# Routed rows gathered a unit ahead, and one PSUM bank of the attention read by two engines

## The chip, the cores and the metric

The kernel runs on one core of one Trainium2 chip. The metric is device time in microseconds (us). Before the change three runs took 1354.52, 1353.81 and 1352.93 us, with a median of 1353.81 us. A separate profiled execution, from which every duration below is read, took 1352.68 us.

## The reference

One input `x` (2048 tokens of 448 numbers) goes through two branches that are mixed per token:

```python
g = _sigmoid((x * gate_w).sum(-1, keepdims=True))
a = _A_ref(x, A_wqkv, A_wo)          # attention, 16 heads of 28
b = _B_ref(x, B_w_gate, B_w1, B_w2)  # 8 experts, the 2 best of each token
return g * a + (1 - g) * b
```

`_A_ref` is full softmax attention over all 2048 keys with an output projection `wo`. `_B_ref` sends each token to two of eight experts (448 to 1792 to 448, with silu) and adds their results with softmax weights.

## The kernel before, in words

The program has four stages on one core. First q, k and v, the routing and the gate are computed. Then the eight experts run; beside them VectorE takes maxima of score tiles. The experts' results go to a tensor `ys_d` in HBM, in the order of the experts' slots. The third stage, from about 836 to 1311 us, is the attention itself. The fourth projects the attention's output with `wo`, adds the routed part and stores it.

The change is in the third stage. There are 16 units `u` (four groups of four heads, times four chunks of 512 queries), and each unit has 8 cells `p`, so 128 cells `m`. A cell handles two tiles of 128 keys for four heads: 8 score tiles of 128 x 512, each the size of one PSUM bank. The scores of cell 0 are made at the end of the expert stage, those of the other 127 by `scores` (L1161).

PSUM has eight banks of that size, and all are in use: two banks of three (`s0`, `s1`, from `triple`) and two single ones (`z0`, `z1`, from `single`). Each cell's `scores` fills, for its first key tile, a single bank and `s0`, and for its second the three banks of `s1` and the other single one. `z[0]` is the single bank of the first key tile, `z[1]` that of the second. ScalarE then computes `exp` into the tile `P` in SBUF: from `z[0]` (L1173), from `s0` (L1174) and from `s1` (L1176). VectorE copies `z[1]` to the SBUF tile `X` (L1175), and ScalarE takes its last `exp` from there (L1177).

`values(m)` (L1180) multiplies the 8 tiles of `P` with the values, 16 matmuls in the trace, into one single bank, and VectorE adds that bank to `osb` (L1192 for the first cell of a unit, L1194 for the others). The bank for this is `single(m + 1)`: the one that held `z[0]` of cell `m + 1`.

The order of each engine's instructions is the order in which the Python code issues them. The loop issues `scores(m + 1)`, then `beside(m)`, then `values(m)`. The tile framework adds the semaphore waits that the order of issue calls for. So on TensorE the scores of the next cell stand ahead of the values of this one, and on VectorE the copy to `X` of the next cell stands ahead of what `beside(m)` puts there and of the add to `osb`.

`beside(m)` spreads the small work over the cells of a unit. In cell 1 `fetch_routed(u)` (L1060) lets GpSimd gather, by two indirect DMAs, the two expert results of 128 tokens out of `ys_d` into `yg0` and `yg1` (two buffers each). `routed(u)` (L1073 to L1077) adds them on VectorE in four steps, in cells 2, 4, 5 and 6. In cell 0 GpSimd's queue also has `collect_sums` of the unit before, in cell 3 `invert_sums` and in cell 4 `spread_sums`; `divide` in cell 7 sends the finished rows to `OT` through SyncE's queue. `split_o` (three VectorE instructions: L1086, L180, L181) prepares tiles of `OT` for the projection; it runs in the cells listed in `WHOLE_O`, and the fourth tile is split by ScalarE after the loop.

Of the kernel before, what the change touches and what calls it, by code (L numbers as in the profile page):

```python
# [8 lines left out]
F32 = mybir.dt.float32  # L9
# [3 lines left out]
AF = mybir.ActivationFunctionType  # L13
# [36 lines left out]
SCALE = float(DH) ** -0.5  # L50
# [12 lines left out]
def tile_gated_mha_moe(ctx: ExitStack, tc: tile.TileContext, x, xe_, xT, wv, wqk, wo, w1, w2, out):  # L63
    nc = tc.nc
# [43 lines left out]
    def max_stream():  # L108
# [6 lines left out]
        while b < len(cells):  # L115
# [19 lines left out]
            if more:  # L135
                nc.vector.tensor_reduce(mp[:, o:o + 1], banks[0], axis=AX.X, op=ALU.max)  # L136
            o += more
# [3 lines left out]
            for lo, hi in zip(cuts, cuts[1:]):  # L141
                h = lo // 3
                nc.vector.tensor_reduce(mp[:, (o + lo) % 256:(o + lo) % 256 + hi - lo], pm[h][:, lo - 3 * h:hi - 3 * h],  # L143
                                        axis=AX.X, op=ALU.max)
            for n, (g, qt, kc, j) in enumerate(step):
                if kc == 3 and j == 3 and qt % 4 == 3:
# [3 lines left out]
                    nc.vector.tensor_reduce(mg[:, 0:16].rearrange("p (j t) -> p j t", j=4), part,  # L150
                                            axis=AX.X, op=ALU.max)
                    mr = mxp.tile([128, 32], F32, name="mr")
# [124 lines left out]
    with ExitStack() as pa:  # L277
        sb = pa.enter_context(tc.tile_pool(name="pa_sb", bufs=1))
# [148 lines left out]
        def tmp(name, shape, dt=F32):  # L427
            return sb.tile(shape, dt, name=name)
# [5 lines left out]
        def routing():  # L434
            Lx = L
            ms_, masks = [], []
            for tag in "12":
                m = tmp("m" + tag, [128, NT])
                nc.vector.tensor_reduce(m, Lx, axis=AX.X, op=ALU.max)
                yield  # L440
# [6 lines left out]
                mi = tmp("mi", [128, NT])  # L447
                nc.vector.tensor_reduce(mi, cand, axis=AX.X, op=ALU.min)
                yield
# [37 lines left out]
            pos = tmp("pos", [128, E])  # L487
            nc.vector.tensor_reduce(pos, ahead, axis=AX.X, op=ALU.add)
            yield
# [199 lines left out]
    def load_v(g, hf):  # L689
        t = cpool[hf].tile([128, NT // 2, 128], F32, name=f"V{hf}")  # L690
        nc.sync.dma_start(t, v_d[hf * 1024:(hf + 1) * 1024, g * 128:(g + 1) * 128]
                          .rearrange("(t p) d -> p t d", p=128))
        return t


    def load_k(g, hf):
        r = []
        cs = slice(hf * 1024, (hf + 1) * 1024)
        for part, src in (("h", qkh_d), ("l", qkl_d)):
            kt_ = cpool[hf].tile([128, 1024], F32R, name=f"K{part}{hf}")  # L700
            kf = kt_.bitcast(F32)
            for j in range(4):
                r0 = D + (4 * g + j) * DH
                nc.sync.dma_start(kf[32 * j:32 * j + DH].rearrange("p (c n) -> p c n", c=2),
                                  src[2 * hf:2 * hf + 2, r0:r0 + DH].rearrange("c r n -> r c n"))
                if part == "h":
                    nc.sync.dma_start(kf[32 * j + DH:32 * j + KR], neg_d[:, cs])
            r.append(kt_)
        return r


    def load_q(g, qc):
        need_max(g, qc)
        q = c0.tile([128, 2, 512], F32R, name="Q", bufs=2)
        qf = q.bitcast(F32)
        for i, src in enumerate((qkh_d, qkl_d)):
            for j in range(4):
                r0 = (4 * g + j) * DH
                nc.sync.dma_start(qf[32 * j:32 * j + DH, i], src[qc, r0:r0 + DH])
        for j in range(4):  # L720
            nc.sync.dma_start(qf[32 * j + DH:32 * j + KR, 0], m_d[4 * g + qc, j:j + 1])
        return q
# [4 lines left out]
    def score_passes(kt, keys, q, banks):  # L727
        kh, kl = keys
        ks = slice((kt % 8) * 128, (kt % 8 + 1) * 128)
        for i, (k, c, r) in enumerate(((kh, 0, KR), (kh, 1, DH), (kl, 0, DH))):  # L730
            for j in range(4):
                rw = slice(32 * j, 32 * j + r)
                nc.tensor.matmul(banks[j], k[rw, ks], q[rw, c], start=i == 0, stop=i == 2)  # L733
# [4 lines left out]
    with ExitStack() as pb:  # L738
        sb1 = pb.enter_context(tc.tile_pool(name="pb_sb1", bufs=2, reuse_waits="tile"))
        sb = pb.enter_context(tc.tile_pool(name="pb_sb", bufs=2, reuse_waits="tile"))  # L740
# [135 lines left out]
        def first_scores(n):  # L876
# [9 lines left out]
            for j in range(4):  # L886
                P = (mxp.tile([128, 512], F32R, name="khg", bufs=6) if 4 * n + j < 6 else
                     mxp.tile([128, 512], F32R, name="qg")).bitcast(F32)
                nc.scalar.activation(P, banks[j], AF.Exp, scale=SCALE)
                Ps[n].append(P)  # L890

# [8 lines left out]
        for e in range(E):  # L900
# [12 lines left out]
            for hf in range(2):  # L913
# [3 lines left out]
                for f in range(NH):  # L917
                    ft = hf * NH + f
                    p = e * NP + ft // 2
# [69 lines left out]
                for n_k, k in enumerate((4, 0, 1, 2, 3)):  # L989
# [7 lines left out]
                    n = 128  # L997
# [3 lines left out]
                    i = 0  # L1001
                    for f in range(NH if k < 4 else 0):
# [10 lines left out]
                        if hf == 1 and e + 1 < E and (f == 1 or f == 4 and n_k == 1):  # L1013
                            j = n_k if f == 1 and n_k > 1 else f // 4
# [27 lines left out]
    sb = ctx.enter_context(tc.tile_pool(name="pc_sb", bufs=2, reuse_waits="tile"))  # L1042
# [8 lines left out]
    def fetch_wo(b):  # L1051
        wo_r[b] = sb.tile([128, D], F32, name="wo_r")
        nc.sync.dma_start(wo_r[b], wo[:, b])

    def split_wo(b):
        w_ = wo_r[b]
        nc.vector.tensor_copy(wo_h[:, b], w_)
        nc.vector.tensor_tensor(wo_l[:, b], w_, wo_h[:, b].bitcast(F32), op=ALU.subtract)

    def fetch_routed(t):  # L1060
        yg = []
        for c in range(2):
            y = sb.tile([128, 2, D], F32, name=f"yg{c}")
            nc.gpsimd.indirect_dma_start(out=y.rearrange("p c d -> p (c d)"), out_offset=None, in_=ys_d,
                                         in_offset=bass.IndirectOffsetOnAxis(ap=slot_i[:, c, t:t + 1], axis=0))
            yg.append(y)
        ygs[t] = yg
# [40 lines left out]
    def collect_sums(u):  # L1108
        for j in range(4):
            nc.gpsimd.dma_start(sum_d[u, j:j + 1], accs[u][32 * j + DH:32 * j + DH + 1])  # L1110
        rc[u] = sb.tile([128, 16], F32, name="rc")
        nc.gpsimd.dma_start(rc[u], by_slices(sum_d[u]))

    def invert_sums(u):
        r = rc.pop(u)
        nc.vector.reciprocal(r, r)
        nc.gpsimd.dma_start(by_slices(inv_d[u]), r)
# [25 lines left out]
    NU = 4 * NG  # L1143
# [4 lines left out]
    Pc = {0: Ps[0] + Ps[1]}  # L1148

    def single(i):  # L1150
        return ps.tile([128, 512], F32, name=f"z{i % 2}")

    def triple(i):
        return ps.tile([128, 3, 512], F32, name=f"s{i}")
# [6 lines left out]
    def scores(m):  # L1161
        u, p = divmod(m, NPR)
        if p == 0 and u and u + 1 < NU:
            qs[u + 1] = load_q((u + 1) // 4, (u + 1) % 4)
        X = sb.tile([128, 512], F32, name="X")
        P = sb.tile([128, 8, 512], F32, name="P")
        z, t = [None] * 2, [None] * 2
        for i in range(2):
            kt = 2 * p + i
            z[i], t[i] = single(m + i), triple(i)  # L1170
            three = [t[i][:, j] for j in range(3)]
            score_passes(kt, held[u // 4][0][kt // 8], qs[u], three + [z[i]] if i else [z[i]] + three)
        nc.scalar.activation(P[:, 0], z[0], AF.Exp, scale=SCALE)  # L1173
        nc.scalar.activation(P[:, 1:4], t[0], AF.Exp, scale=SCALE)  # L1174
        nc.vector.tensor_copy(X, z[1])  # L1175
        nc.scalar.activation(P[:, 4:7], t[1], AF.Exp, scale=SCALE)  # L1176
        nc.scalar.activation(P[:, 7], X, AF.Exp, scale=SCALE)  # L1177
        Pc[m] = [P[:, i] for i in range(8)]

    def values(m):  # L1180
        u, p = divmod(m, NPR)
# [14 lines left out]
    def beside(m):  # L1196
        u, p = divmod(m, NPR)
        g, qc = divmod(u, 4)
        if qc == 3 and g + 1 < NG:
            if p == 3:  # L1200
                held[g + 1] = [load_k(g + 1, 0), None], [None, None]
            if p == 4:
                held[g + 1][1][0] = load_v(g + 1, 0)
            if p == 6:
                held[g + 1][0][1] = load_k(g + 1, 1)
        if g and qc == 0 and p == 0:
            held[g][1][1] = load_v(g, 1)
        if u and p == 0:
            collect_sums(u - 1)
        if p == 1:  # L1210
            fetch_routed(u)
        if p == 4 and 4 <= u < 8:
            fetch_wo(u - 4)
        if p == 0 and 5 <= u < 9:
            split_wo(u - 5)
        if (u, p) in WHOLE_O:
            split_o(WHOLE_O.index((u, p)), nc.vector)
        if u and p == 3:
            invert_sums(u - 1)
        if u and p == 4:  # L1220
            spread_sums(u - 1)
        if u and p == 7:
            divide(u - 1)
        if p in (2, 4, 5, 6):
            next(sums.setdefault(u, routed(u)))

    WHOLE_O = [(NU - 2, 1), (NU - 1, 0), (NU - 1, 1)]
    for m in range(NU * NPR):
        if m + 1 < NU * NPR:
            scores(m + 1)  # L1230
        beside(m)
        values(m)
# [70 lines left out]
```

## Time and profile before

| | before |
|---|---|
| median of three runs | 1353.81 us |
| the profiled execution | 1352.68 us, of which the span of its instructions is 1350.9 us |
| TensorE busy | 1341.4 us (99%) |
| VectorE busy | 928.1 us (69%) |
| ScalarE busy | 847.5 us (63%) |
| GpSimd busy | 616.6 us (46%) |
| mean granted TensorE clock | 0.998 of full speed |

Busy time is the time covered by an engine's records. Records of consecutive instructions overlap, on TensorE and on ScalarE alike, and the ends of matmuls are modelled; so a share of 99% does not say that the engine could do no more. In the rows below a start and a duration stand first, and the bracket behind an instruction tells how long its engine had been idle before it and what ended that. PE is TensorE, DVE is VectorE, ACT is ScalarE, POOL is GpSimd.

### The profile page before, as it was taken

The page shows a single profiled execution, that of the slowest core. Times are in us where ns is not written, and L with a number is a line of the kernel's source. Part 1 is how long each engine was busy: PE and PEld are TensorE (multiplying, and loading weights), DVE is VectorE, ACT ScalarE, POOL GpSimd, SP SyncE. Part 2 cuts the span into 40 slices and gives each one's busy share as a digit, 9 for nine tenths or more (in the row PEclk, how much of TensorE's full clock was granted, in tenths as well). Part 3 has the DMA queues.
Part 4 walks back from the last instruction along what each step waited for, and adds up shares of the span by engine and source line. Part 5 has one row for each costly group of instructions (what it writes and reads, how often), then busy time and mean ns, then how long its engine had stood idle before and what let it go on. Part 6 is the DMA issues. An engine that isn't in the chain of part 4 may idle for free. (4 is left out here: it accounts for less than half of the span.)

```text
span 1350.9 us, 27181 instructions
## 1 busy us (share of the span) xinstructions
PE 1341.4 (99%) x10166; PEld 887.2 (66%) x10166; DVE 928.1 (69%) x1076; ACT 847.5 (63%) x1270; POOL 616.6 (46%) x661
## 2 busy tenths in 40 slices
PE   9999999999999999999999999999999999999998
PEld 8888788788887777777777776434444444444348
DVE  5746898888988888988888775444445444444455
ACT  5325354355354343543435435999999999999881
POOL 2123775676587666875768752122222222222220
PEclk9999999999999999999999999999999999999999
DMA  9887856753453465534655313123322432432123
GB/s 344 306 272 263 301 156 192 239 160 104 154 157 104 143 192 160 161 97 144 187 154 162 102 39 103 42 62 106 103 77 71 131 100 58 109 103 70 48 58 129
DMA packets 136279, 191.30 MB, mean 142 GB/s; under 512 B 23285, under 2 KB 102681, under 8 KB 135633
## 3 DMA queue, kind: packets, MB, share of 16 engines
q1 hardware_dynamic: 124992, 160.55, 38.3%
q0 software_dynamic: 11008, 28.76, 7.1%
q8 instruction: 80, 1.31, 0.4%
q14 instruction: 55, 0.44, 0.1%
q10 hardware_dynamic: 144, 0.23, 0.1%
HBM read 139.20 MB, written 60.74 MB: 148 GB/s over the span
## 5 line engine op out<-in xcount | busy, mean ns | idle before, releaser
L143 DVE TENSOR_REDUCE mp<-pm 128x3 f32<-128x1536 f32 (+1 forms) x301 | 508.9, 1733 | 10.9 <-PE pm L122 10.9
L1188 PE MATMUL z<-P,V 128*32 128x512 f32 x2032 | 246.4, 602 | 0.0
L1176 ACT ACTIVATE P<-s 128x1536 f32<-128x1536 f32 x127 | 198.1, 1560 | 0.9 <-PE s L733 0.9
L1174 ACT ACTIVATE P<-s 128x1536 f32<-128x1536 f32 x127 | 196.5, 1547 | 0.0
L1175 DVE COPY X<-z 128x512 f32<-128x512 f32 x127 | 87.9, 692 | 150.2 <-PE z L733 142.1
L733 PE MATMUL s<-Q,Kh 29*128 29x512 f32 x1524 | 188.5, 444 | 0.0
L733 PE MATMUL z<-Q,Kh 29*128 29x512 f32 x508 | 185.5, 444 | 2.7 <-DVE osb L1194 2.7
L804 POOL TENSOR_TENSOR w2l<-w2r,w2h 128x448 fp32r<-128x448 f32 x112 | 129.3, 1156 | 117.9 <-ACT w2h L798 90.4
L1020 ACT ACTIVATE yo<-acc 128x448 f32<-128x448 f32 x64 | 34.8, 544 | 231.1 <-PE acc L1006 226.3
L1006 PE MATMUL acc<-w2h,hh 128*128 128x448 f32 x448 | 167.5, 374 | 0.3 <-PEq L818 0.3
L1006 PE MATMUL acc<-w2h,hl 128*128 128x448 f32 x448 | 166.4, 372 | 0.0
L1006 PE MATMUL acc<-w2l,hh 128*128 128x448 f32 x448 | 166.0, 371 | 0.0
L949 ACT ACTIVATE hf<-acc 128x512 f32<-128x512 f32 (+6 forms) x154 | 74.2, 482 | 138.0 <-PE acc L945 131.0
L733 PEld LDWEIGHTS z<-Q,Kh 29*128 29x128 f32 x508 | 74.5, 183 | 111.9 <-issue 30.2
L136 DVE TENSOR_REDUCE mp<-acc 128x1 f32<-128x512 f32 x130 | 89.5, 688 | 84.6 <-PE pm L122 81.6
L813 POOL TENSOR_TENSOR hl<-hf,hh 128x512 fp32r<-128x512 f32 x112 | 144.9, 1294 | 1.0 <-ACT hh L952 1.0
L1188 PEld LDWEIGHTS z<-P,V 128*32 128x32 f32 x2032 | 53.3, 109 | 129.7 <-issue 77.4
L945 PE MATMUL acc<-xeh,w1h 128*128 128x512 f32 (+3 forms) x408 | 136.8, 339 | 0.0
L945 PE MATMUL acc<-xeh,w1l 128*128 128x512 f32 (+3 forms) x408 | 136.0, 338 | 0.0
L1194 DVE TENSOR_TENSOR osb<-z,osb 128x512 f32<-128x512 f32 x112 | 77.4, 691 | 82.1 <-PE z L1188 81.9
L1110 POOL DMA_DIRECT2D sum_d<-osb x64 | 31.0, 492 | 202.8 <-DVE osb L1194 202.8
L772 POOL TENSOR_TENSOR w1l<-w1r,w1h 128x1024 fp32r<-128x1024 f32 (+1 forms) x49 | 90.9, 1854 | 61.1 <-ACT w1h L766 47.5
(221 smaller groups left out, 2779.1 us busy)
## 6 DMA issues: line engine op xcount, KB each, us to landing
w2r<-in_w_dram SPq DMA_DIRECT2D x112, 224.0 KB
w1r<-in_w_dram SPq DMA_DIRECT2D x56, 384.0 KB
ys_d<-zero_d SPq DMA_DIRECT2D x32, 448.0 KB
ys_d<-yo SPq DMA_DIRECT2D x64, 224.0 KB
x_d<-xf SPq DMA_DIRECT2D x115, 64.0 KB
qkh_d<-hi SPq DMA_DIRECT2D x28, 256.0 KB
qkl_d<-lo SPq DMA_DIRECT2D x28, 256.0 KB
w1r<-in_w_dram SPq DMA_DIRECT2D x112, 64.0 KB
```

The source lines that it names most:

```text
L136: nc.vector.tensor_reduce(mp[:, o:o + 1], banks[0], axis=AX.X, op=ALU.max)
L143: nc.vector.tensor_reduce(mp[:, (o + lo) % 256:(o + lo) % 256 + hi - lo], pm[h][:, lo - 3 * h:hi - 3 * h], axis=AX.X, op=ALU.max)
L733: nc.tensor.matmul(banks[j], k[rw, ks], q[rw, c], start=i == 0, stop=i == 2)
L772: nc.gpsimd.tensor_tensor(l[:, :, half], r[:, :, half], h[:, :, half].bitcast(F32), op=ALU.subtract)
L804: nc.gpsimd.tensor_tensor(w2l, w2r, w2h.bitcast(F32), op=ALU.subtract)
L813: nc.gpsimd.tensor_tensor(hl, hf32, hh[:, 0:512].bitcast(F32), op=ALU.subtract)
L945: nc.tensor.matmul(pu[:, 0:HC], a, b[:, cs], start=i == 0, stop=i == len(mms) - 1)
L1006: nc.tensor.matmul(py[:n, 0:D], a[:, cs], b, start=i == 0, stop=i == 3 * NH - 1)
L1174: nc.scalar.activation(P[:, 1:4], t[0], AF.Exp, scale=SCALE)
L1175: nc.vector.tensor_copy(X, z[1])
L1176: nc.scalar.activation(P[:, 4:7], t[1], AF.Exp, scale=SCALE)
L1188: nc.tensor.matmul(po[32 * j:32 * j + 32], v[:, kt % 8, 32 * j:32 * j + 32], P[4 * i + j], start=i == 0, stop=i == 1)
```

## The change

There are three edits, all in the attention stage.

1. `z[0]` of every cell is read by two engines. ScalarE takes `exp` of its columns 0 to 255 straight from the bank; VectorE copies its columns 256 to 511 to the front of `X`, which grows from 512 to 768 columns. The copy of `z[1]` goes behind it in `X`, and ScalarE's last `exp` takes all 768 columns of `X`. The order of issue is: ScalarE's `exp` of the half bank, VectorE's copy of the other half, the two `exp` of 1536 columns, VectorE's copy of `z[1]`, the last `exp`. `P` becomes one row of 4096 columns, in which columns 0 to 511 are the first score tile and columns 512 to 1023 the one that comes from `z[1]`.
2. The gathers of a unit are issued in cell 5 of the unit before, those of unit 0 ahead of the loop.
3. Three `split_o` move from cells (14, 1), (15, 0), (15, 1) to cells (15, 0), (15, 1), (15, 3), as (unit, cell).

```diff
-        X = sb.tile([128, 512], F32, name="X")
-        P = sb.tile([128, 8, 512], F32, name="P")
+        X = sb.tile([128, 768], F32, name="X")
+        P = sb.tile([128, 4096], F32, name="P")
...
-        nc.scalar.activation(P[:, 0], z[0], AF.Exp, scale=SCALE)
-        nc.scalar.activation(P[:, 1:4], t[0], AF.Exp, scale=SCALE)
-        nc.vector.tensor_copy(X, z[1])
-        nc.scalar.activation(P[:, 4:7], t[1], AF.Exp, scale=SCALE)
-        nc.scalar.activation(P[:, 7], X, AF.Exp, scale=SCALE)
-        Pc[m] = [P[:, i] for i in range(8)]
+        nc.scalar.activation(P[:, 0:256], z[0][:, 0:256], AF.Exp, scale=SCALE)
+        nc.vector.tensor_copy(X[:, 0:256], z[0][:, 256:512])
+        for i in range(2):
+            nc.scalar.activation(P[:, 1024 + 1536 * i:2560 + 1536 * i], t[i].rearrange("p j n -> p (j n)"),
+                                 AF.Exp, scale=SCALE)
+        nc.vector.tensor_copy(X[:, 256:768], z[1])
+        nc.scalar.activation(P[:, 256:1024], X, AF.Exp, scale=SCALE)
+        Pc[m] = [P[:, 512 * i:512 * i + 512] for i in (0, 2, 3, 4, 5, 6, 7, 1)]
...
-        if p == 1:
-            fetch_routed(u)
+        if p == 5 and u + 1 < NU:
+            fetch_routed(u + 1)
...
-    WHOLE_O = [(NU - 2, 1), (NU - 1, 0), (NU - 1, 1)]
+    fetch_routed(0)
+    WHOLE_O = [(NU - 1, 0), (NU - 1, 1), (NU - 1, 3)]
```

## Rows read from the trace of the kernel before

**Rows 1.** An undisturbed stretch of the attention as one window: its length, then the busy time of PE, PEld (weight loads), DVE, ACT and POOL with the number of instructions, the granted clock, the share of the DMA engines and GB/s.

```profile
1010.00:1200.00 190.00, 190.00 (x2072) 77.11 (x2068) 91.76 (x147) 190.00 (x208) 46.93 (x79) 1.00 0.35 96
```

**Rows 2.** ScalarE's instructions in order of time, in an undisturbed stretch of the attention.

```profile
1102.77 0.72 ACT L1173 ACTIVATE P<-z 128x512 f32<-128x512 f32 x1
1103.26 1.57 ACT L1174 ACTIVATE P<-s 128x1536 f32<-128x1536 f32 x1
1104.59 1.58 ACT L1176 ACTIVATE P<-s 128x1536 f32<-128x1536 f32 x1
1105.92 0.76 ACT L1177 ACTIVATE P<-X 128x512 f32<-128x512 f32 x1
1106.45 0.72 ACT L1173 ACTIVATE P<-z 128x512 f32<-128x512 f32 x1
...
1128.57 0.72 ACT L1173 ACTIVATE P<-z 128x512 f32<-128x512 f32 x1
```

**Rows 3.** TensorE and VectorE beside the same cell: the values, the copy to X, the first and the last matmul of the next z[0], the add to osb.

```profile
1103.54 1.92 PE L1188 MATMUL z<-P,V 128*32 128x512 f32 x16
1103.66 0.69 DVE L1175 COPY X<-z 128x512 f32<-128x512 f32 x1 [1.12 <-PE z L733]
1105.39 0.49 PE L733 MATMUL z<-Q,Kh 29*128 29x512 f32 x1
1105.53 0.69 DVE L1192 COPY osb<-z 128x512 f32<-128x512 f32 x1 [1.18 <-PE z L1188]
1105.96 0.39 PE L733 MATMUL z<-Q,Kl 28*128 28x512 f32 x1
```

**Rows 4.** All instructions of L1173 in the program: shortest, median and longest duration in ns, first and last start.

```profile
L1173 ACT ACTIVATE P<-z x127: 597/714/723, 835.9 to 1306.2; 128x512 f32<-128x512 f32 x127
```

**Rows 5.** Waits from 880 to 1320 us: engine, what waited, for whom, us in total, times, the longest in us. Below them the gathers' time from issue to landing, and one pair of gathers in GpSimd's order of time.

```profile
DVE yg L1073 <- DMA yg<-ys_d,slot_i: 6.5, 7, 2.0
DVE oh L1086 <- DMA OT<-osb: 2.1, 1, 2.1
...
DMA to landing us min/median/max: 4.1/4.9/6.9
...
960.17 0.97 POOL L1064 DMA_INDIRECT yg<-ys_d,slot_i  x1 [0.31 <-issue]
```

**Rows 6.** Two of those waits in order of time, and what follows on TensorE and ScalarE; below them the window in which the granted clock was lowest.

```profile
964.81 0.62 DVE L1073 TENSOR_TENSOR yg<-yg 128x448 f32<-128x448 f32 x1 [1.97 <-DMA yg<-ys_d,slot_i]
965.36 0.68 DVE L1194 TENSOR_TENSOR osb<-z,osb 128x512 f32<-128x512 f32 x1
966.09 0.49 PE L733 MATMUL z<-Q,Kh 29*128 29x512 f32 x1 [0.88 <-DVE osb L1194]
969.91 0.60 ACT L1173 ACTIVATE P<-z 128x512 f32<-128x512 f32 x1 [1.05 <-PE s L733]
...
1259.96 0.49 PE L733 MATMUL z<-Q,Kh 29*128 29x512 f32 x1 [1.85 <-DVE osb L1194]
1260.75 1.45 ACT L1176 ACTIVATE P<-s 128x1536 f32<-128x1536 f32 x1 [0.86 <-PE s L733]
1260.86 3.62 PE L1188 MATMUL z<-P,V 128*32 128x512 f32 x16
1265.46 0.60 ACT L1173 ACTIVATE P<-z 128x512 f32<-128x512 f32 x1 [2.74 <-PE s L733]
...
1261.00:1262.00 1.00, 1.00 (x8) 0.25 (x8) 0.96 (x2) 1.00 (x1) 0.00 (x0) 0.50 0.00 0
```

**Rows 7.** TensorE after the second of these waits: the first matmul of a cell's scores, and the values behind them.

```profile
1264.41 0.49 PE L733 MATMUL z<-Q,Kh 29*128 29x512 f32 x1
1266.18 1.92 PE L1188 MATMUL z<-P,V 128*32 128x512 f32 x16
```

**Rows 8.** The first stage, in order of time: ScalarE (L416) reads columns 0 to 447 of a PSUM bank, VectorE (L417) columns 448 to 456 of the same bank; the two pairs are of two banks.

```profile
14.37 0.55 ACT L416 ACTIVATE hi<-pq 128x448 f32<-128x448 f32 x1 [2.65 <-PE pq L371]
14.81 0.54 ACT L416 ACTIVATE lo<-pq 128x448 f32<-128x448 f32 x1
14.95 0.17 DVE L417 COPY lg<-pq 128x9 f32<-128x9 f32 x1 [2.33 <-ACT hi L416]
15.38 0.17 DVE L417 COPY lg<-pq 128x9 f32<-128x9 f32 x1 [0.26 <-ACT lo L416]
```

**Rows 9.** Groups by line and shape: busy us and mean ns of one, for reads out of PSUM of other widths, for the copy to X, and for the three instructions of split_o (the last three lines; these from 880 to 1320 us).

```profile
L274 ACT ACTIVATE xeh<-pt 128x256 fp32r<-128x256 f32 x1 | 0.4, 380 | 0.0
...
L581 DVE COPY dg<-pt 128x128 f32<-128x128 f32 x1 | 0.3, 281 | 0.0
...
L1175 DVE COPY X<-z 128x512 f32<-128x512 f32 x127 | 87.9, 692 | 150.2 <-PE z L733 142.1 <-PE s L733 8.1
...
L180 DVE TENSOR_TENSOR ol<-OT,oh 128x384 fp32r<-128x384 f32 x7 | 3.9, 556 | 0.1
...
L181 DVE TENSOR_TENSOR oh<-OT,oh 64x128 fp32r<-64x128 f32 x7 | 2.0, 290 | 0.2
...
L1086 DVE CAST oh<-OT 128x512 fp32r<-128x512 f32 x3 | 1.4, 463 | 2.1 <-DMA OT<-osb 2.1
```

**Rows 10.** The end of the loop in order of time: ScalarE's last exp, the first matmul of the projection.

```profile
1309.32 0.73 ACT L1177 ACTIVATE P<-X 128x512 f32<-128x512 f32 x1
...
1311.08 0.47 PE L1097 MATMUL s<-wo_h,oh 128*128 128x448 f32 x1
```

## The prediction, made before the changed kernel ran

> **What bounds the kernel now.** I read the page's busy time first (the table above). It names TensorE (99%) and gives ScalarE only 63%, but that is a mean over stages. A window in the attention, where all edits lie, shows TensorE and ScalarE without a gap: 190.00 of 190.00 us each [rows 1]. Records overlap, so this doesn't say which of the two ends last. The timeline of ScalarE does. From the start of one L1173 to the next but six, 1102.77 to 1128.57, seven cells take 25.80 us, 3.686 us each [rows 2]. The starts inside a cell are 0.49, 1.33, 1.33 and 0.53 us apart, while one instruction lasts 0.2 to 0.25 us longer than that [rows 2]: the next one is always there before the last has drained. A cell's L1173 lasts 0.72 us here and 0.60 us behind a wait [rows 2, 6]; the difference is queueing in ScalarE. So ScalarE sets the pace, 3.686 us for 4096 columns in four instructions.
>
> TensorE is close behind. After a wait, when nothing of ScalarE holds it, it goes from the first score matmul of a cell to the values in 1.77 us (1264.41 to 1266.18) [rows 7], and from the values to the next scores in 1.85 us (1103.54 to 1105.39) [rows 3]: 3.62 us. Two more things are to be seen. The values can't start before L1173 of the next cell ends (1102.77 + 0.72 = 1103.49, values at 1103.54) [rows 2, 3], since they need its bank. And L1173 starts 0.10 us after z[0]'s last matmul ends (1105.96 + 0.39 = 1106.35; 1106.45) [rows 2, 3]. Those two make a ring: scores to exp, exp to values, values to the next scores. With an unqueued exp it would take 1.06 + 0.60 + 0.05 + 1.85 = 3.56 us, so today it has 0.13 us to spare against ScalarE.
>
> The pace is lost in places. First to last L1173 is 1306.2 - 835.9 = 470.3 us [rows 4]; 126 cells at 3.686 are 464.4. So 5.9 us are waits. VectorE stands in its queue until a gather has landed (seven times, up to 2.0 us) or until OT has landed (2.1 us, once) [rows 5]; the add to osb behind it is late, so is the bank that TensorE needs, and ScalarE then idles 1.05 us at 969.91, and 0.86 and 2.74 us at 1260.75 and 1265.46 [rows 6]. The last is the dearest, since after TensorE had stood 1.85 us its granted clock was 0.50 (1.2 GHz) and 16 matmuls took 3.62 us for 1.92 [rows 6].
>
> **The change, part by part.** *Gathers a unit ahead.* The same 32 instructions of about 1 us on GpSimd. They land 4.1 to 6.9 us after issue [rows 5]; from cell 5 to cell 2 of the next unit are five cells, 18 us, so no wait on them is left. On GpSimd they leave the place ahead of L1117 and come behind the four DMAs of spread_sums; the next work in that queue is collect_sums three cells later, 11 us for 2 us of gathers. The two buffers they write were last read a unit ago. Unit 0's gathers need the last rows of ys_d and can't come earlier by being issued earlier. *split_o later.* The three instructions move half a unit and more behind the transfer they stood waiting for; they last 0.46 + 0.56 + 0.29 us [rows 9], and VectorE has 1.18 us idle ahead of the add [rows 3], so some 0.2 us of an add's lateness is added, which is about TensorE's spare time. Both edits together give back the 5.9 us of waits, as long as nothing else is late.
>
> *ScalarE's four instructions.* 256 + 1536 + 1536 + 768 columns are the 4096 of before in as many instructions. 512 columns take 0.49 us from the bank and 0.53 from X [rows 2], so moving 256 of them changes 0.02 us a cell either way. ScalarE's own pace stays 3.69.
>
> *The half bank.* This is the term that decides. VectorE's new copy reads the bank that ScalarE's half exp reads, and is issued behind it. Does it run beside it or after it? The trace has one place of the kind: L416 and L417 read different columns of one bank, with no data between them. VectorE, idle for 2.33 us, starts at 14.95 when ScalarE has ended at 14.92; for the next bank, idle again, it starts at 15.38 and ScalarE ended at 15.35 [rows 8]. It waits for ScalarE each time. So I take the two reads as one after the other, and VectorE's copy then stands between the exp and the values, which need the whole bank free. The ring becomes:
> - first score matmul to exp: 1106.45 - 1105.39 = 1.06 us [rows 2, 3];
> - exp of 256 columns, unqueued: 0.38 us (L274 has 0.380 for this width [rows 9]; 0.60 for 512);
> - ScalarE's end to VectorE's start: 0.03 us [rows 8];
> - copy of 256 columns: the trace has 0.281 us for 128 and 0.692 for 512 [rows 9]. These are its bounds; on the line between them 256 columns take 0.281 + 0.411 x 128/384 = 0.42 us;
> - VectorE's end to TensorE: 0.05 us (965.36 + 0.68 = 966.04; 966.09 [rows 6]);
> - values to next scores: 1.85 us.
>
> Together 3.79 us. That is more than ScalarE's 3.69, so the ring takes the pace and ScalarE idles 0.10 us in each cell. Behind the waiting copy VectorE has the copy of z[1], the small work and the add; z[1] is ready only about 0.9 us after the half exp started, so none of these is late, and it is TensorE alone that waits. 126 cells at 3.79 are 477.5 us, 7.2 more than the 470.3 of now, waits included. By the bounds of the copy the ring is 3.65 (ScalarE keeps the pace: 464.4 us, 5.9 less) or 4.06 (511.6, 41.3 more).
>
> The Trainium skill (PSUM — Partial Sum Buffer, Specifications (TRN2)) says that ScalarE and VectorE can read PSUM in parallel at full bandwidth unless they collide in a bank; its section on bank collisions counts different columns of one bank as a collision, and reads against reads too. By the first sentence alone the copy would hide beside the exp and the time would be that of the first rival below; by the second the program must keep the two apart, as L417 does here [rows 8], and the sum stands.
>
> *The tail.* Now the last cell's values wait for L1177 with their last matmuls only, and the projection starts at 1311.08, 4.89 us after the last L1173 [rows 4, 10]. Afterwards the first score tile, with which the values begin, has its second half from the last exp. That ends at 0.27 + 1.33 + 1.33 + 0.83 = 3.76 us after the last half exp began (0.83 is 0.62 unqueued plus 256 columns); then 0.05 and 16 matmuls of 1.85: 5.66 us, 0.77 more than now. The projection behind it is untouched.
>
> Sum against the profiled execution: 1352.68 + 7.2 + 0.8 = 1360.7 us. The median of the runs stands 1.1 us above that execution, so the forecast is 1361.8, rounded to 1362 us: slower by 0.6%.
>
> **The rivals.**
> - *The two reads run side by side.* Then the bank is free 0.1 us after the half exp could have freed it at the earliest, the ring stays under 3.56 us, ScalarE keeps the pace at 3.686, and the waits are gone: -5.9 + 0.8, so 1348.7 us, faster. It decides as soon as VectorE's copy starts before L1173 ends. For it: nothing in the data makes the copy wait. Against it: rows 8. 10%.
> - *They follow each other, but the ring is shorter than my sum,* by 0.03 to 0.10 us a cell, so that it ends near ScalarE's pace: 1349 to 1357. The widths of copy and exp are interpolated; but the line has rows on both sides. 7%.
> - *Waits stay.* Another late DMA takes the place of the gathers, or split_o in cell (15, 3), with the reciprocal behind it, holds the add; in a ring without spare time 5.9 us of it go on top: 1367.7. I see no such transfer. 6%.
> - *TensorE's clock.* It would now stand about 0.18 us a cell, and 1.1 us before the last values. Only the 1.85 us wait was followed by the level of 1.2 GHz, not the 0.88 us one [rows 6]. If it fell once in a unit, 16 times 1.7 us come on top: 1389. 3%.
>
> **How the numbers follow.** My own case has 74% and reaches from 1357 to 1367 (0.03 us a cell either way, and the tail). The range is 1353 to 1369 us: it adds the upper half of the second rival and nearly all of the third, some 83%; the first rival and the clock stay outside. A measurement of this kernel can tell about 0.2% from no change, that is 1351.1 to 1356.5. Faster: the first rival and a part of the second, 12%. Same: 5%. Slower: 83%.
>
> **What would show it.** VectorE's 256-column copy starts 0.03 us behind the end of each half exp; the values start 0.05 us behind that copy; L1173's successor lasts 0.38 us, with some 0.1 us idle ahead of it in every cell; from one to the next it is 3.79 us. No wait on yg or OT is left in the loop, and the clock stays at 1.00 there. The prediction is wrong if the copy overlaps the half exp, or if the cells stay at 3.69 us.

## The result, and the profile after

The changed kernel takes 1363.59 us (median of four runs, 1362.63 to 1364.03) against 1353.37 us for the kernel before, which ran with it (four runs, 1349.34 to 1354.52). The ratio is 1.0082, with a 95% interval of 1.0067 to 1.0097: slower by 0.8%. The forecast was 1362 us, in a range of 1353 to 1369 us. The profiled execution took 1363.72 us with a span of 1361.9 us, 11.0 us more than before.

The page of the changed kernel, its busy time and its chain of waits:

```profile
PE 1340.4 (98%) x10166; PEld 904.0 (66%) x10166; DVE 979.5 (72%) x1203; ACT 861.2 (63%) x1270; POOL 616.8 (45%) x661
...
ACT 33%; PE 7%; DVE 0%; issue 0%; ACTq 0%; DVEq 0%
ACT P L1176 23%; ACT P L1179 6%; ACT P L1173 4%; PE z L1190 2%; PE s L1097 1%; PE acc L1006 1%; PE z L1097 1%; PE z L733 1%; DVE X L1174 0%; PE pm L733 0%; PE s L733 0%; PE pm L122 0%; PE acc L122 0%; DVE b L1100 0%; ACTq L1084 0%
```

By this page nothing seems to have moved to VectorE: the chain goes through ScalarE (33%) and gives the new copy L1174 0%. The window that answers to [rows 1] tells a little more:

```profile
1010.00:1200.00 190.00, 184.58 (x2000) 81.75 (x1996) 109.89 (x194) 189.47 (x201) 42.86 (x72) 1.00 0.33 91
```

TensorE, without a gap before, now has 5.42 us of gaps in 190 us, at a granted clock of 1.00. ScalarE still shows 189.47 of 190.00. The timeline of one cell, to be set beside [rows 2, 3] (L1173 is the half exp, L1174 the new copy, L1176 the two long exps, L1179 the exp of `X`, L1190 the values):

```profile
1101.92 0.50 PE L733 MATMUL z<-Q,Kh 29*128 29x512 f32 x1
...
1102.11 0.86 ACT L1179 ACTIVATE P<-X 128x768 f32<-128x768 f32 x1
...
1102.98 0.39 ACT L1173 ACTIVATE P<-z 128x256 f32<-128x256 f32 x1
...
1103.26 2.79 ACT L1176 ACTIVATE P<-s 128x1536 f32<-128x1536 f32 x2
...
1103.40 0.42 DVE L1174 COPY X<-z 128x256 f32<-128x256 f32 x1 [0.65 <-ACT P L1173]
...
1103.80 0.69 DVE L1178 COPY X<-z 128x512 f32<-128x512 f32 x1
1103.87 0.16 PEld L1190 LDWEIGHTS z<-P,V 128*32 128x32 f32 x8 [0.55 <-DVE X L1174]
1103.87 1.92 PE L1190 MATMUL z<-P,V 128*32 128x512 f32 x16
...
1105.73 0.49 PE L733 MATMUL z<-Q,Kh 29*128 29x512 f32 x1
...
1105.92 0.86 ACT L1179 ACTIVATE P<-X 128x768 f32<-128x768 f32 x1
```

The ring can be read off: from the first score matmul to the half exp 1.06 us (1101.92 to 1102.98), the exp 0.39, then 0.03 to VectorE's copy, the copy 0.42, 0.05 to the values (1103.87), and 1.86 to the next score matmul (1105.73): 3.81 us for a cell, 3.686 before. VectorE stands idle 0.65 us ahead of the copy, for L1173, and the first weight load of the values stands 0.55 us for the copy.

All instructions of L1173, to be set beside [rows 4], with who waited for them:

```profile
L1173 ACT ACTIVATE P<-z x127: 384/385/386, 835.9 to 1316.4; 128x256 f32<-128x256 f32 x127
...
  DVE X L1174: 82.0, 126
```

First to last takes 480.5 us, 10.2 more than before, and VectorE waited for the half exp in each of the 126 cells of the loop. The waits from 880 to 1320 us, and the gathers' time from issue to landing, beside [rows 5]:

```profile
DVE X L1174 <- ACT P L1173: 74.8, 115, 0.9
PEld z L1190 <- DVE X L1174: 63.2, 115, 0.8
...
DMA to landing us min/median/max: 4.0/4.2/4.3
```

The waits on yg and the wait of L1086 on OT are gone. The end of the loop, beside [rows 10]:

```profile
1316.40 0.39 ACT L1173 ACTIVATE P<-z 128x256 f32<-128x256 f32 x1
...
1319.34 0.85 ACT L1179 ACTIVATE P<-X 128x768 f32<-128x768 f32 x1
...
1320.25 1.92 PE L1190 MATMUL z<-P,V 128*32 128x512 f32 x16 [1.03 <-ACT P L1179]
...
1322.10 0.47 PE L1097 MATMUL s<-wo_h,oh 128*128 128x448 f32 x1
```

From the last L1173 to the projection it is 5.70 us (1316.40 to 1322.10), 0.8 more than before. 10.2 + 0.8 = 11.0 us: the whole difference of the spans lies in these two places.

### The profile page after: what moved, and what is told of

Same layout as the page of the kernel before. It is cut to its first block, busy times and chain, and to the rows that moved or that the text cites. A ratio compares the mean times of both kernels' runs of the same rounds, so it can differ in the third digit from the quotient of the medians.

```text
span 1361.9 us, 27226 instructions
## 1 busy us (share of the span) xinstructions
PE 1340.4 (98%) x10166; PEld 904.0 (66%) x10166; DVE 979.5 (72%) x1203; ACT 861.2 (63%) x1270; POOL 616.8 (45%) x661
## 5 line engine op out<-in xcount | busy, mean ns | idle before, releaser
L1176 ACT ACTIVATE P<-s 128x1536 f32<-128x1536 f32 x254 | 354.2, 1451 | 0.0
L1190 PE MATMUL z<-P,V 128*32 128x512 f32 x2032 | 244.3, 598 | 15.0 <-ACT P L1179 1.0
L733 PE MATMUL s<-Q,Kh 29*128 29x512 f32 x1524 | 175.2, 419 | 0.0
L1190 PEld LDWEIGHTS z<-P,V 128*32 128x32 f32 x2032 | 53.0, 109 | 147.1 <-issue 76.0
L1174 DVE COPY X<-z 128x256 f32<-128x256 f32 x127 | 53.9, 425 | 89.7 <-ACT P L1173 82.0
L122 PE MATMUL pm<-khg,qg 28*128 28x512 f32 x894 | 110.4, 449 | 0.9 <-DVE lo L645 0.9
```

The lines of the kernel that those rows point to most:

```text
L122: nc.tensor.matmul(banks[n], qgs[g, qt // 4][rw, (qt % 4) * 128:(qt % 4 + 1) * 128], kh[g, kc][rw], start=True, stop=True)
L1176: nc.scalar.activation(P[:, 1024 + 1536 * i:2560 + 1536 * i], t[i].rearrange("p j n -> p (j n)"), AF.Exp, scale=SCALE)
L1190: nc.tensor.matmul(po[32 * j:32 * j + 32], v[:, kt % 8, 32 * j:32 * j + 32], P[4 * i + j], start=i == 0, stop=i == 1)
```

## The experiments

The theory was that the bank which two engines read one after the other closes a ring of 3.81 us, and that this ring has taken the pace from ScalarE. Its rival was that ScalarE still sets the pace, now at 3.81 us, as its records without a gap and the page's chain say. The kernels ran in four sessions on three chips, each beside the kernel before, whose median there was 1351.9, 1357.5, 1356.0 and, again on the first chip, 1352.0 us; so kernels of different sessions are compared by their ratio to it. "First to last" is L1173's, 126 cells.

### Edits 2 and 3 alone

```diff
-        if p == 1:
-            fetch_routed(u)
+        if p == 5 and u + 1 < NU:
+            fetch_routed(u + 1)
...
-    WHOLE_O = [(NU - 2, 1), (NU - 1, 0), (NU - 1, 1)]
+    WHOLE_O = [(NU - 1, 0), (NU - 1, 1), (NU - 1, 3)]
+    fetch_routed(0)
```

> Edits 2 and 3 alone (gathers a unit ahead, split_o later), z[0] read by ScalarE alone as before. Ring theory: ScalarE keeps its 3.686 us a cell, the 5.9 us of waits are gone and nothing else changes, 1347.5 us (1346 to 1349.5), no wait on yg or OT in the loop. Rival, that another late transfer takes the place of the gathers: within 2 us of the kernel before, 1352 to 1354.

1346.62 us, ratio 0.9963 (0.9950 to 0.9977). All instructions of L1173 in it:

```profile
L1173 ACT ACTIVATE P<-z x127: 597/717/724, 834.9 to 1299.7; 128x512 f32<-128x512 f32 x127
```

First to last is 464.8 us, next to the 464.4 of 126 cells at 3.686: the waits on yg and of L1086 on OT are gone, and 5.5 of the 5.9 us came back. These two edits are a gain by themselves, which the half bank hides.

### Edit 1 alone

```diff
-        nc.scalar.activation(P[:, 0], z[0], AF.Exp, scale=SCALE)
...
+        nc.scalar.activation(P[:, 0:256], z[0][:, 0:256], AF.Exp, scale=SCALE)
+        nc.vector.tensor_copy(X[:, 0:256], z[0][:, 256:512])
...
+        nc.vector.tensor_copy(X[:, 256:768], z[1])
+        nc.scalar.activation(P[:, 256:1024], X, AF.Exp, scale=SCALE)
```

> Edit 1 alone (z[0] read by both engines), gathers and split_o where they were. Ring theory: 3.81 us a cell as in the changed kernel, and the waits on yg and OT come on top, since a ring without spare time gives nothing back: 1365 to 1370 us. Rival, that the slower cells give the gathers time to land: the changed kernel's 1363.6.

1366.72 us, ratio 1.0113 (1.0098 to 1.0129). A cell takes 3.81 us, and the old waits are back:

```profile
DVE yg L1073 <- DMA yg<-ys_d,slot_i: 4.8, 6, 1.5
DVE oh L1086 <- DMA OT<-osb: 2.4, 1, 2.4
```

First to last is 483.4 us (835.1 to 1318.5): 480.4 for 126 cells, and 3.0 us of waits. So edit 1 alone costs 1.1%, and in the changed kernel the other two edits take some 0.3% of that off again.

### The copy from the other bank

In the changed kernel the 256-column copy takes its columns from `z[1]`. ScalarE's instructions, their widths and VectorE's work are the same; only the bank `z[0]` has one reader again.

```diff
-        nc.vector.tensor_copy(X[:, 0:256], z[0][:, 256:512])
+        nc.vector.tensor_copy(X[:, 0:256], z[1][:, 256:512])
```

> The changed kernel, with VectorE's 256-column copy taken from z[1] and not from z[0]: every instruction keeps its engine, size and place, only the shared bank is gone (the second half of each first score tile is left out, columns of z[1] stand in its place). Ring theory: the values need ScalarE's half exp alone, the ring has time to spare, ScalarE's own pace of 3.69 us a cell sets the time: 1348 to 1349.5 us. Rival, that ScalarE itself needs 3.81 us for 256, 1536, 1536 and 768 columns (its records follow each other with 0.01 us between them in the changed kernel): 1363.6, no change.

1348.46 us (ten runs, 1347.83 to 1349.26), ratio 0.9977 (0.9967 to 0.9986). The rival, no change from the changed kernel's 1.0082, falls. The values wait for the half exp again, and no longer for the copy (from 880 to 1320 us); below that, ScalarE's timeline in it:

```profile
PEld z L1190 <- ACT P L1173: 46.5, 111, 0.4
...
1099.58 1.19 ACT L1179 ACTIVATE P<-X 128x768 f32<-128x768 f32 x1
1100.34 0.72 ACT L1173 ACTIVATE P<-z 128x256 f32<-128x256 f32 x1
1100.62 3.12 ACT L1176 ACTIVATE P<-s 128x1536 f32<-128x1536 f32 x2
1103.28 1.19 ACT L1179 ACTIVATE P<-X 128x768 f32<-128x768 f32 x1
1104.03 0.72 ACT L1173 ACTIVATE P<-z 128x256 f32<-128x256 f32 x1
```

The same four instructions now take 3.69 us from one L1173 to the next. Set beside the changed kernel's rows above, the starts of L1173, L1176 and L1179 are the same distances apart (0.28 and 2.66 us); only from L1179 to the next L1173 it is 0.75 us here and 0.87 there. That 0.12 us is ScalarE's wait. No gap shows there because an instruction's record lasts beyond the point at which a queued successor starts: the half exp starts 0.44 us before L1179's record ends here (1103.28 + 1.19 = 1104.47, against 1104.03), and 0.01 us behind its end in the changed kernel. The durations show it better than the gaps: 0.72 and 1.19 us queued, 0.39 and 0.86 not.

### VectorE takes both banks whole

If the bank has one reader only, one step drops out of the ring: a single copy stands where the exp and the copy stood. Here VectorE copies all of `z[0]` (L1173 in this kernel) and `z[1]`, and ScalarE has 1536 + 1536 + 1024 columns.

```diff
-        nc.scalar.activation(P[:, 0:256], z[0][:, 0:256], AF.Exp, scale=SCALE)
-        nc.vector.tensor_copy(X[:, 0:256], z[0][:, 256:512])
+        nc.vector.tensor_copy(X[:, 0:512], z[0])
...
-        nc.vector.tensor_copy(X[:, 256:768], z[1])
-        nc.scalar.activation(P[:, 256:1024], X, AF.Exp, scale=SCALE)
+        nc.vector.tensor_copy(X[:, 512:1024], z[1])
+        nc.scalar.activation(P[:, 0:1024], X, AF.Exp, scale=SCALE)
```

> The changed kernel, but VectorE copies all of z[0] as well as z[1] to X (1024 columns), and ScalarE has three instructions: 1536, 1536, 1024. No bank is read by two engines. Ring theory: 0.96 for z[0], 0.11 to VectorE's start, 0.69 copy, 0.05, 1.86 values: 3.67 us a cell; ScalarE alone would need 3.63. So the ring sets the pace and the time is 1345 to 1347.5 us, below the kernel before. Rival, that ScalarE's own pace follows its columns and instructions only as in the rival of the run above (0.28 + 0.87 for 1024 columns): 3.8 us a cell, 1362.

1356.31 us, ratio 1.0038 (1.0024 to 1.0052), 3.766 us a cell: a miss, above the kernel before and not below it. The timeline of a cell, and TensorE's semaphore instructions ahead of the values, in this kernel:

```profile
1100.91 1.06 ACT L1178 ACTIVATE P<-X 128x1024 f32<-128x1024 f32 x1
...
1101.95 0.69 DVE L1173 COPY X<-z 128x512 f32<-128x512 f32 x1 [0.25 <-PE s L733]
...
1102.76 0.19 PEld L1189 LDWEIGHTS z<-P,V 128*32 128x32 f32 x8 [0.47 <-issue]
...
1102.79 1.92 PE L1189 MATMUL z<-P,V 128*32 128x512 f32 x16
...
L1189 PEldq EVENT_SEMAPHORE  x126: 51/51/895, 839.3 to 1309.7; - x126
```

The same row of the changed kernel:

```profile
L1190 PEldq EVENT_SEMAPHORE  x7: 51/51/51, 851.0 to 1217.2; - x7
```

The copy ends at 1102.64. The weight load starts 0.12 us later and the first matmul 0.15 us later, for 0.05 us in the changed kernel. The first values matmul uses the tile of `P` that ScalarE's last exp writes, and the bank that the copy frees. That exp (L1178) isn't late: it ends at 1101.97, 0.67 us before the copy. In the changed kernel the copy itself has waited for a later instruction of ScalarE, so a wait for the copy covers both; here the copy waits for no exp, and the matmul needs a wait for each engine. In 126 cells TensorE's queue has a separate semaphore instruction of 51 ns or more there; in the changed kernel in 7.

### The same, with the late tile last

The values begin with heads 1 to 3, so that the matmul which closes the ring needs only the bank.

```diff
-            for j in range(4):
+            for j in ((0, 1, 2, 3) if i or u == p == 0 else (1, 2, 3, 0)):
```

> The kernel in which VectorE copies both single banks, with one change: in each cell but the first the values' matmuls of a key tile with heads 1, 2, 3 are issued ahead of head 0. The first weight load then waits for VectorE's copy alone and not also for ScalarE's exp of X. Ring theory, with the 0.10 us that the trace of that kernel shows between the copy's end and the values (0.15 for 0.05, a separate 51 ns semaphore instruction among it) put down to that second wait: 3.67 us a cell for 3.77, 1343 to 1346 us. Rival, that the 0.10 us belong to the wide copy or to the bank: 1356, no change.

1351.03 us, ratio 0.9959 (0.9945 to 0.9974), 3.665 us a cell. In its trace:

```profile
1102.30 0.69 DVE L1173 COPY X<-z 128x512 f32<-128x512 f32 x1 [0.22 <-PE s L733]
...
1103.05 0.16 PEld L1189 LDWEIGHTS z<-P,V 128*32 128x32 f32 x8 [0.38 <-DVE X L1173]
...
L1189 PEldq EVENT_SEMAPHORE  x8: 51/51/51, 855.4 to 1306.0; - x8
```

The semaphore instructions are gone but for 8, the weight load starts 0.06 us behind the copy (1102.99), and a cell takes 0.10 us less. The order of the matmuls was the only edit, and the exp had ended before the copy in either case, so the 0.10 us belong to the second wait on the first of them; in 126 cells it makes 12.6 us, which covers the miss. The cell came out as forecast. The 1343 to 1346 us were counted from a chip on which the kernel before takes 1351.9 us, and so stand for a ratio of 0.9934 to 0.9956; the measured one lies just above, with an interval that covers most of it. In its trace the first cells of the loop lose 1.8 us (see below), and seven later cells lose 0.05 to 0.31 us each, the cause of which isn't settled.

### The half bank copied twice

The 256-column copy is issued twice, which adds one copy to the ring.

```diff
-        nc.vector.tensor_copy(X[:, 0:256], z[0][:, 256:512])
+        for _ in range(2):
+            nc.vector.tensor_copy(X[:, 0:256], z[0][:, 256:512])
```

> The changed kernel, with VectorE's 256-column copy of z[0] issued twice. Ring theory: the second copy stands in the ring with its whole issue distance, some 0.35 to 0.42 us in each of 126 cells: 4.16 to 4.23 us a cell, 1407 to 1417 us. Rival, that ScalarE's own pace sets the 3.81 us: the second copy has room beside it and the time stays at 1363 to 1366.

1438.94 us, ratio 1.0609 (1.0580 to 1.0639), 4.366 us a cell: the direction was right, the size too small. In its timeline:

```profile
1103.11 0.39 ACT L1173 ACTIVATE P<-z 128x256 f32<-128x256 f32 x1 [0.57 <-PE s L733]
...
1103.53 0.88 DVE L1175 COPY X<-z 128x256 f32<-128x256 f32 x2 [0.66 <-ACT P L1173]
...
1104.53 0.19 PEld L1191 LDWEIGHTS z<-P,V 128*32 128x32 f32 x8 [1.08 <-issue]
1104.56 1.92 PE L1191 MATMUL z<-P,V 128*32 128x512 f32 x16 [0.68 <-DVE X L1175]
...
L1191 PEldq EVENT_SEMAPHORE  x127: 51/51/1495, 840.4 to 1393.7; - x127
```

The two copies take 0.88 us, and the values start 0.15 us behind them, again with a semaphore instruction in every cell. The second copy needs no wait of its own for the half exp, as it stands behind the first; so the second wait is most likely TensorE's own for the half exp. The trace's list of who waited for L1173 has the values' weight loads 122 times, besides the copies. With both terms the ring is 1.06 + 0.39 + 0.03 + 0.88 + 0.15 + 1.86 = 4.37 us, as measured. Here ScalarE's wait is long enough to show as a gap, 0.57 us ahead of L1173.

### Edit 2 alone, edit 3 alone

Each is the half of the first experiment's diff that its name says.

> Edit 2 alone (gathers a unit ahead). By the trace of the kernel before, 1.9 of the 5.9 us lost in the loop follow waits on yg; 1350 us, and the wait on OT with its low clock stays. Rival, that the gathers also stand in the way of other transfers and so cause the wait on OT: 1347.

> Edit 3 alone (split_o later). 3.8 of the 5.9 us follow the wait on OT and the low clock behind it: 1348 to 1349 us, waits on yg stay. The two edits alone should add up to what they bring together.

Edit 3 alone: 1353.23 us, ratio 0.9974 (0.9960 to 0.9989), about 3.5 us of 1357.5 (1.5 to 5.4 by the interval); the wait of L1086 is gone, those on yg stay. Edit 2 alone: 1355.46 us, ratio 0.9995 (0.9979 to 1.0010); the 1.9 us expected lie within the interval, and so does no gain at all, so the time tells nothing. Whether the two add up to what they bring together can't be told from such intervals either. The trace of edit 2 alone has no wait on yg, and the wait of L1086 stays (2.1 us, once), so its rival, that the gathers cause that wait, falls. But it has a loss near the start of the loop. GpSimd's gathers and two windows (columns as in [rows 1]):

```profile
840.18 0.96 POOL L1064 DMA_INDIRECT yg<-ys_d,slot_i  x1 [21.45 <-DMA wo_r<-in_wo_dram]
841.44 0.95 POOL L1064 DMA_INDIRECT yg<-ys_d,slot_i  x1 [0.30 <-issue]
842.70 0.95 POOL L1064 DMA_INDIRECT yg<-ys_d,slot_i  x1 [0.30 <-issue]
843.95 0.94 POOL L1064 DMA_INDIRECT yg<-ys_d,slot_i  x1 [0.30 <-issue]
...
840.00:848.00 8.00, 6.62 (x68) 2.91 (x64) 2.08 (x3) 7.18 (x9) 3.81 (x4) 0.94 0.75 241
848.00:850.00 2.00, 2.00 (x13) 0.59 (x16) 1.22 (x2) 1.90 (x3) 0.00 (x0) 0.50 0.19 72
```

The same windows of edit 3 alone:

```profile
840.00:848.00 8.00, 8.00 (x95) 3.52 (x91) 3.64 (x6) 8.00 (x11) 1.51 (x2) 1.00 0.37 117
848.00:850.00 2.00, 2.00 (x28) 0.61 (x20) 0.69 (x1) 2.00 (x4) 0.00 (x0) 1.00 0.00 0
```

GpSimd, which has nothing to wait for in its queue, issues unit 1's gathers directly behind unit 0's. In that stretch the DMA share is 0.75 for 0.37, TensorE stands for 1.38 us of the 8, and the granted clock is 0.50 (1.2 GHz) afterwards.

### Does the first gather cost something?

First the two best versions again on a third chip, then unit 1's gathers put back to where they were, beside edits 2 and 3 on the first chip:

```diff
+        if p == 1 and u == 1:
+            fetch_routed(u)
-        if p == 5 and u + 1 < NU:
+        if p == 5 and 1 <= u < NU - 1:
             fetch_routed(u + 1)
```

> The kernel of gather_and_split, beside the next one on one chip. Ratio to the kernel before 0.995 to 0.997; ScalarE at 3.686 us a cell.

> The kernel of both_banks_order, beside the one above on one chip. By 3.665 against 3.686 us a cell it would be 2.6 us less in the loop; the 0.3 us that its trace loses once a unit (some 4 us) and a later start of the projection take that back. So within 3 us of the one above, on either side; both below the kernel before.

> Edits 2 and 3, but unit 1's gathers stay in cell 1 of their unit; those of units 2 to 15 come a unit ahead. Theory: GpSimd has nothing to wait for in unit 0 and issues unit 1's gathers right behind unit 0's, beside the loads of the second half of the keys and values (DMA share 0.84 to 0.93); where they collide, some 1.5 to 3 us are lost in the first three cells. Without that, 1 to 3 us below the next kernel on the same chip, and no interval over 3.9 us ahead of 850 us. Rival, that those first cells lose their time to something else: the same time within 1 us.

> The kernel of gather_and_split once more, beside the one above on one chip. Ratio to the kernel before 0.995 to 0.998.

On the third chip edits 2 and 3 alone had 0.9977 (0.9968 to 0.9986) and VectorE with both banks and the new order 0.9966 (0.9952 to 0.9979): the intervals overlap, so neither is shown to be the better. On the first chip the first gather put back had 0.9955 (0.9942 to 0.9969), and edits 2 and 3 unchanged 0.9956 (0.9943 to 0.9970): no difference, where the theory had forecast 1 to 3 us. The latter's window on that chip:

```profile
840.00:848.00 8.00, 8.00 (x90) 3.20 (x89) 3.63 (x6) 8.00 (x10) 2.40 (x3) 1.00 0.67 226
```

There TensorE and ScalarE lost nothing, at a DMA share of 0.67 with the early gathers in it. The loss of 1 us and more showed in the traces of two other chips only: in all five traces with the early gathers there (TensorE busy for 6.62 to 6.71 of the 8 us in four of them, and for 5.67 in the kernel with two copies), and not in that of edit 3 alone, which lacks them. The fall of the clock behind it showed in edit 2 alone only; in the other four it was 1.00 from 848 to 850 us. The edit against the loss was not run on these chips. Whether the early gathers cause it stays open. Edits 2 and 3 without the half bank were faster than the kernel before in all three of their sessions, by 0.2 to 0.4%.

## Why the prediction was right

*The half bank.* Right, by its own mechanism. The copy waits for the half exp in every cell, and the ring of six terms sets the pace. The Trainium skill (PSUM — Partial Sum Buffer, PSUM bank collisions raise a hardware error) asks the program to keep two engines apart by bank rather than by address; the trace agrees: L1174 waited for L1173 in each of the 126 cells. So the serial order is shown as what the program's waits do; what two reads of one bank at the same time would cost on the chip, no run here shows. That the ring sets the pace is shown from two sides: without the shared bank the pace falls back to 3.69 us, and a second copy in the ring lengthens the cell by 0.55 us. The sum was 3.79 us and the ring 3.81: exp 0.385 for 0.38, copy 0.425 for 0.42, values 1.86 for 1.85, and roundings. Over 126 cells this makes 480.4 for 477.5 us, nearly all of the 3.0 us by which the profiled execution (1363.72) lies above the sum (1360.7). The median lies only 1.6 us above the forecast, since it stands 0.1 us below its profiled execution and not the 1.1 us above that was carried over from before. That these two errors cancel in part is luck.

*Gathers and split_o.* Right as to the waits: none on yg or of L1086 is left, and the two edits together gave back 5.5 of the 5.9 us in the kernel with one reader. How this splits is shown in part only: edit 3 gave some 3.5 us, and of the gathers alone no gain in time is shown. A loss near 845 us, seen in the traces of two chips, was not foreseen.

*ScalarE's own pace.* Right: 3.69 us with the new widths, in the kernel that copies from the other bank.

*The tail.* 5.70 us for the predicted 5.66.

*The clock.* It stayed at 1.00 in the loop, although TensorE now stands 0.11 us in a cell (5.42 us in the 50 cells of the window), less than the 0.18 us of the prediction.

*What would show it.* One sign was wrong: "some 0.1 us idle ahead of it in every cell" can't be seen in the records, as L1179's unqueued record reaches to 0.01 us before the half exp. The page's chain therefore names ScalarE, and it took a kernel with the same ScalarE work and another bank to tell the two apart.

The rival of side-by-side reads fell with the 0.03 us between L1173's end and the copy's start; the copy from the other bank, which has no such wait, comes near its 1348.7 us (a ratio of 0.9962 to the 1353.8 of before; measured 0.9977, 0.9967 to 0.9986). The rival of waits that stay is the kernel with edit 1 alone; there they cost 3.0 us and not the 5.9 us that the rival put on top. The other two did not occur.

## What to carry to other kernels

Before half of a PSUM bank is moved to a second engine, add up the ring that this bank closes: where the second read can only follow the first, the split lengthens the time that the bank is held, and where the first engine keeps its total of work, nothing can be gained for it. Of an engine whose records touch, read the durations: where they are as short as behind a wait (here 0.39 and 0.86 us, for 0.72 and 1.19 when queued), the engine has spare time, whatever the chain of waits names. Give the instruction that closes the ring one wait only, and put what needs a second engine behind it.

## What the runs showed that was not expected

- A second wait on the instruction that closes the ring costs 0.10 us a cell: the weight load starts 0.12 us behind the copy for 0.06, and the first matmul later again. Another order of the same matmuls takes it back (3.766 to 3.665 us).
- ScalarE's records can cover 189.47 of 190.00 us while it waits 0.12 us in every cell.
- The same kernel's median was 1351.9 us on one chip and 1357.5 on another, and a loss near the start of the loop appeared on some of them only.
